# A dense block's second product by seven block products instead of eight, with the halves of its middle layer outermost

## The chip, the core and the metric

The kernel runs on one core of a Trainium2 chip. The metric is the device time of one execution in microseconds. The engines of the core are TensorE (PE: matrix products; PEld is its loading of weights), VectorE (DVE), ScalarE (ACT), GpSimd (POOL) and SyncE (SP), which here only starts DMA transfers. Each engine works through its own queue in program order and waits at semaphores for the others.

## What is computed

Two layers, each an attention block and a dense block, on 2048 rows of 640 numbers in float32; both layers use the same weights:

```
def _A_ref(x, wqkv, wo):            # 32 heads of 20
    q, k, v = heads of (x @ wqkv)
    p = softmax(q k^T * 20 ** -0.5)
    return (p v, heads side by side) @ wo

def _B_ref(x, w1, b1, w2, b2):      # w1: 640 x 1536, w2: 1536 x 640
    h = x @ w1 + b1
    r = where(h > 0, h, 0)
    return (r * r) @ w2 + b2

x = x + _A_ref(layernorm(x), wqkv, wo)
x = x + _B_ref(layernorm(x), w1, b1, w2, b2)
x = x + _A_ref(layernorm(x), wqkv, wo)
x = x + _B_ref(layernorm(x), w1, b1, w2, b2)
```

## The kernel before, in words

Every matrix product of float32 numbers is made of three products: a number is split in a high part, rounded for TensorE (type `F32R`), and a low part, the rest; high x high, high x low and low x high are added up (`THREE`). A split (`split_to`, L269 and L270) is a copy on ScalarE that rounds, and a subtraction on VectorE that gives the rest. The weights are split once, on GpSimd (`pool_hi`, `pool_lo`, L284 and L289), during the attention of the first layer: `prep_job` is called at three of each 16 steps of attention, and the split weights go to DRAM and are loaded again in each layer (`Split`).

The order of work on each engine is the order in which the program writes the instructions down (`manual_schedule`). What belongs to something else than the product in hand is written in between by hand: the dense block calls `side()` after each piece of its work, and each call takes one entry off the list `steps`, which `layer` fills from `plan`.

The **dense block** (`mlp`) is called once for each of four blocks of 512 rows (`qb`). The rows come normalised, transposed and split: `xnt`, five tiles. The middle layer of 1536 columns is worked on in two halves (`fh`) of six chunks of 128. For each half:

- First product: for each of six chunks 15 matmuls of 512 columns (`chain`, L306), ScalarE adds the bias and cuts below zero (L1363), VectorE squares (L1364), and the square is split (L269, L270) into one tile `h`.
- During the first half, the four tiles of 128 rows of `x_mid` are loaded and GpSimd adds the bias `b2` to them (L1370).
- Second product: for each of four row tiles and two halves of the 640 output columns, 6 chunks x 3 matmuls of 320 columns (L1378) into one bank of PSUM, which VectorE then adds to the row tile (L1389). After the second half the row tile is stored.

So the work goes block by block, and both halves of the middle layer follow each other for one block. I call the work of one block and one half a group; there are eight in each layer. All of the second product's weights (`w_2`, 16 tiles) and the first's (`w_1`, 15 tiles) stay loaded. Tiles come from an arena of 42 (`NSLOT`), and rows and intermediate results from a pool of 11 (`NX`). PSUM has 8 banks, used in turn (`ps_all`).

Beside this, by way of `plan`, the next block's rows are **turned**: `turn_out` loads its four row tiles, takes their statistics (VectorE, L257 and L258; GpSimd adds and takes the power, L260 and L261), normalises (L265), transposes blocks of 32 (L1318) and stores them to `d_t`; `turn_in` loads them transposed and splits them (L1334 on ScalarE, L1335 on VectorE). In the first layer the results of the dense block are turned too, for the next layer's attention (`ahead`).

What comes ahead of the dense block, `add_heads`, multiplies the heads by `wo` (L306) and stores `x_mid`; meanwhile the weights of the dense block are loaded, and block 0 is turned.

## Time and profile before

| | us |
|---|---|
| median of 3 runs | 3478.88 (3478.14 to 3479.41) |
| the profiled execution | 3476.63 |
| its span in the profile | 3474.8 |
| dense block of the first layer, in the span | 1414.1 to 1746.4 |
| dense block of the second layer, in the span | 3139.2 to 3471.5 |

How to read the views that follow. The page begins with the busy time of each engine, its share of the span and its instructions. A group of instructions by line shows: the line, the engine, the operation, what it writes and reads, shapes, the count; then busy time and the mean length of one in ns; then the idle time of the engine just before these instructions and what ended it ("<-" is the releaser). A row of the timeline is: start, length, engine, line, operation, tiles, how many instructions are merged in it, and in brackets the idle time before it with its releaser. A row of the chain of waits is: start, length, engine, what, how many. A row of a table of stretches is: from and to, length, then the busy time and the number of instructions of PE, PEld, DVE, ACT and POOL, the clock that TensorE was granted (1.00 is full), the busy share of the DMA engines and GB/s.

### The profile page before, as it was taken

How to read it: one execution, taken by the hardware profiler on the slowest of the kernel's cores; microseconds unless marked ns; L12 is line 12 of the kernel's file. 1: busy time of each engine (PE TensorE's matmuls, PEld its weight loads, DVE VectorE, ACT ScalarE, POOL GpSimd, SP SyncE). 2: the span in 40 equal slices, each digit the busy share in tenths (PEclk: the TensorE clock that was granted, in tenths of full speed). 3: DMA queues.
4: the chain of work that ended last, by engine and by line, in shares of the span. 5: the costliest groups of instructions: out<-in, count | busy, mean ns of one | idle time of the engine just before them, and what ended most of it. 6: DMA issues, size and time to landing. Idle time of an engine off the chain costs nothing.

```text
span 3474.8 us, 69900 instructions
## 1 busy us (share of the span) xinstructions
PE 3458.5 (100%) x26490; PEld 2178.2 (63%) x26490; DVE 2745.0 (79%) x5085; ACT 2595.7 (75%) x4170; POOL 814.8 (23%) x940
## 2 busy tenths in 40 slices
PE   9999999999999999999999999999999999999999
PEld 7897444444444446999989964444444444479998
DVE  8888999999999992456568889999999999834443
ACT  3778999999999994222237799999999999932221
POOL 6531444221121121111153201221121121111110
PEclk9999999999999999999999999999999999999999
DMA  9866555322211146734477552222232111376230
GB/s 309 281 232 185 173 163 162 119 62 80 67 52 44 38 121 214 251 106 108 137 269 260 192 154 78 69 79 70 65 83 58 51 48 43 119 245 221 80 83 36
DMA packets 377138, 452.24 MB, mean 130 GB/s; under 512 B 176612, under 2 KB 223716, under 8 KB 376800
## 3 DMA queue, kind: packets, MB, share of 16 engines
q1 hardware_dynamic: 375984, 445.40, 41.9%
q8 instruction: 208, 3.41, 0.4%
q10 hardware_dynamic: 816, 2.36, 0.2%
q14 instruction: 130, 1.06, 0.1%
HBM read 273.34 MB, written 174.30 MB: 129 GB/s over the span
## 4 chain that ended last, share of the span: by engine, by line
PE 97%; DMA 1%; DVE 1%; issue 0%; ACT 0%; POOL 0%; SPq 0%; DVEq 0%; POOLq 0%; ACTq 0%
PE banks L635 29%; PE banks L494 19%; PE banks L621 14%; PE banks L306 13%; PE banks L344 11%; PE banks L1378 10%; PE banks L1219 0%; PE banks L421 0%; ACT e L1226 0%; DVE bst L257 0%; SPq L76 0%; DMA x<-d_x 0%; DMA d_m<-mr 0%; DMA o<-d_r 0%; DMA b_t<-in_B_b_dram 0%
## 5 line engine op out<-in xcount | busy, mean ns | idle before, releaser
L506 DVE TENSOR_REDUCE mx<-banks 128x1 f32<-128x512 f32 x2096 | 1428.7, 686 | 136.0 <-PE banks L494 30.5
L494 PE MATMUL banks<-k,q 60*128 60x512 f32 (+1 forms) x4488 | 1311.3, 370 | 1.9 <-DVE v L390 1.9
L494 PEld LDWEIGHTS banks<-k,q 60*128 60x128 f32 x4488 | 714.5, 184 | 832.0 <-DVE mx L541 725.9
L629 ACT ACTIVATE e<-banks 128x512 f32<-128x512 f32 x1988 | 1195.4, 602 | 13.2 <-PE banks L621 2.2
L635 PE MATMUL banks<-e,vg 128*32 128x512 f32 x8192 | 1093.5, 606 | 1.5 <-ACT e L1226 1.5
L621 PE MATMUL banks<-q,k 62*128 62x512 f32 x3968 | 1072.5, 421 | 0.6 <-DVE mx L562 0.6
L631 ACT ACTIVATE e<-banks 128x1024 f32<-128x1024 f32 x990 | 1007.9, 1018 | 0.0
L541 DVE TENSOR_REDUCE mx<-banks 128x2 f32<-128x512 f32 x928 | 633.0, 682 | 3.4 <-PE banks L494 3.4
L621 PEld LDWEIGHTS banks<-q,k 62*128 62x128 f32 x3968 | 580.3, 184 | 53.8 <-ACT e L629 52.8
L562 DVE CUSTOM_DVE_ANT_0 rl<-banks,rl 128x512 f32<-128x512 f32 x536 | 349.7, 689 | 78.8 <-PE banks L494 60.1
L1363 ACT ACTIVATE r<-banks,b_t 128x512 f32<-128x512 f32 x96 | 66.1, 689 | 416.4 <-PE banks L306 415.0
L344 PE MATMUL banks<-xnT,wqk 64*128 64x512 f32 x2400 | 372.5, 393 | 0.3 <-ACT mark_t L346 0.3
L554 ACT ACTIVATE rl<-banks 128x512 f32<-128x512 f32 x538 | 295.4, 595 | 102.2 <-PE banks L494 85.0
L1378 PE MATMUL banks<-w,h 128*128 128x320 f32 x2304 | 340.4, 309 | 0.0
L1378 PEld LDWEIGHTS banks<-w,h 128*128 128x128 f32 x2304 | 339.2, 188 | 1.2
L306 PE MATMUL banks<-xnT,w 128*128 128x512 f32 x1440 | 329.4, 389 | 0.0
L635 PEld LDWEIGHTS banks<-e,vg 128*32 128x32 f32 x8192 | 161.7, 108 | 258.7 <-issue 254.9
L344 PEld LDWEIGHTS banks<-xnT,wqk 64*128 64x128 f32 x2400 | 294.0, 186 | 30.5 <-issue 2.3
L306 PEld LDWEIGHTS banks<-xnT,w 128*128 128x128 f32 x1440 | 269.7, 188 | 55.2
L284 POOL CAST mr<-nt 128x32 fp32r<-128x32 f32 x64 | 13.4, 210 | 1096.2 <-DVE nt L588 1096.2
L679 POOL TENSOR_TENSOR few<-few,minus_t 128x16 f32<-128x16 f32 x62 | 179.8, 2900 | 189.4 <-DMA few<-d_s 175.1
L344 PE MATMUL banks<-wv,xnT 64*128 64x320 f32 x1920 | 209.8, 308 | 0.8 <-ACT mark_t L346 0.8
(90 smaller groups left out, 2343.4 us busy)
## 6 DMA issues: line engine op xcount, KB each, us to landing
q<-d_qk SPq DMA_DIRECT2D x240, 240.0 KB
d_qk<-ev SPq DMA_DIRECT2D x80, 512.0 KB
k<-d_qk SPq DMA_DIRECT2D x152, 240.0 KB
x<-d_x SPq DMA_DIRECT2D x84, 320.0 KB
d_qk<-ev SPq DMA_DIRECT2D x80, 256.0 KB
d_o<-ot SPq DMA_DIRECT2D x248, 80.0 KB
ot<-d_o SPq DMA_DIRECT2D x38, 512.0 KB
d_v<-v SPq DMA_DIRECT2D x32, 512.0 KB
```

The source lines that it names most:

```text
L306: nc.tensor.matmul(dst, a, b, start=(n == 0), stop=(n == last))
L344: m = nc.tensor.matmul(ch["dst"][:, :width], *pair, start=first, stop=last)
L494: return nc.tensor.matmul(dst, q_t[t][b : b + 60, p, sub * P : (sub + 1) * P], k_t[t // NQB, c][b : b + 60, p, keys], start=True, stop=True,)
L506: nc.vector.tensor_reduce(maxima(t)[:, 2 * par + p, sub, c : c + 1], dst, axis=AX.X, op=ALU.max)
L541: r = nc.vector.tensor_reduce(maxima(t)[:, p : p + 3 : 2, sub, c if not half else column(t, p, sub)], bank.rearrange("q (r k) -> q r k", r=2),
L554: nc.scalar.activation(res, dst, AF.Relu)
L562: nc.vector.tensor_tensor_reduce(out=r, in0=dst, in1=r, scale=1.0, scalar=LEAST, op0=ALU.add, op1=ALU.max, accum_out=maxima(t)[:, 2 * par ...
L621: nc.tensor.matmul(dst, k_t[t // NQB, kt // 4][b : b + 62, p, (kt % 4) * P : (kt % 4 + 1) * P], q_t[t][b : b + 62, p, :], start=True, stop ...
L629: nc.scalar.activation(es[h], dst, AF.Exp, scale=SCALE)
L631: nc.scalar.activation(es[pair], banks[:, 1:3, :], AF.Exp, scale=SCALE)
L635: nc.tensor.matmul(acc[32 * h : 32 * h + 32, :], v_t[t // NQB, kt // 8][:, kt % 8, 32 * h : 32 * h + 32], es[h], start=(kt == 0), stop=(kt ...
L1378: nc.tensor.matmul(dst[:, :HALF], hs[f][:, hx, i * P : (i + 1) * P], w_2.piece(at_2(f0 + f, hw, hf)), start=(f == 0 and (hx, hw) == THREE[0]),
```

## The change

The second product of each group is seen as a product of 2 x 2 blocks: the 512 rows in two halves of 256, the six chunks in three and three, the 640 output columns in 320 and 320. Seven products of blocks (the variant with 4 additions on the left and 4 on the right) replace the eight.

- **Weights** (`Seven` in place of `Split` for `w_2`): for each pair of chunks (f, f + 3) GpSimd makes the four sums of quarter blocks and splits seven operands instead of four, in three calls of `prep_job`; 14 tiles of three pieces for each half of the middle layer go to DRAM. Each half's 14 tiles are loaded in each layer.
- **Left operands** (`left_operands`): after the second chunk of a pair, four additions of 256 columns, on GpSimd for pairs 0 and 1, on VectorE for pair 2, then the splits of a11 (256 columns), of h (the second chunk, 512), of s1 and of s2 (512 each). The first chunk's other half is not split.
- **The product**: three pairs of banks are opened with pairs 0 and 1 of products 0, 1 and 2; then pair 2 of each, and products 3 to 6 are added onto these banks. After each product VectorE adds the bank to the part of the rows where it belongs: 14 additions in a group instead of 8.
- **Order**: `fh` is now the outer loop and the block the inner one. So the rows after the first half are stored to DRAM (`d_half`) and loaded again in the second half; the normalised rows (`xnt`) are stored to `d_xn` and loaded again for the second half (`again`), which does not turn them a second time; only 8 tiles of `w_1` are loaded at the start, the other seven in the last group of the first half, as well as the other half's `w_2`.
- **Turning**: block 1 is turned out during `add_heads`, block 2 during block 0's group of the first half, block 3 during block 1's. In the first layer, blocks 0 to 2 of the result are turned during blocks 1 to 3 of the second half, each row tile after chunks 0, 2 and 4.

The diff, cut to its core:

```
+    class Seven:
+        n = 14
+        wide = 3 * HALF
...
+        def prepared(self, fh, f, top, low):
+            b11, b12 = top[:, :HALF], top[:, HALF:]
+            b21, b22 = low[:, :HALF], low[:, HALF:]
...
+            for dst, a, b in ((t1, b12, b11), (t2, b22, t1), (t3, b22, b12), (t4, b21, t2)):
+                nc.gpsimd.tensor_sub(dst, a, b)
+            halves(1, two(), t1)
+            yield
...
-        + [("2", f) for f in range(NF)]
+        + [("2", f) for f in range(NF // 2)]
...
-    def mlp(qb, xnt, x_mid, x_dst, side, last):
+    def mlp(fh, qb, xnt, x_mid, x_dst, side, last):
...
+        def left_operands(p, r, h):
+            eng = nc.vector if p == 2 else nc.gpsimd
...
+            a11, a21, a12, a22 = r[:, :w], r[:, w:], h[:, :w], h[:, w:]
+            eng.tensor_add(s[:, 0, 0, :], a21, a22)
+            eng.tensor_sub(s[:, 0, 1, :], s[:, 0, 0, :], a11)
+            eng.tensor_sub(s[:, 1, 0, :], a12, s[:, 0, 1, :])
+            eng.tensor_sub(s[:, 1, 1, :], a11, a21)
+            split_to(a[:, 0, :], a[:, 1, :], a11)
+            for x, y in (("h", h), ("s1", s[:, 0]), ("s2", s[:, 1])):
+                x = ops[x, p]
+                y = y if y is h else y.rearrange("p a t -> p (a t)")
+                split_to(x[:, 0, :], x[:, 1, :], y)
+        for n in range(6):
+            p, low = divmod(n, 2)
+            f = fh * 6 + p + 3 * low
...
+            r = xtile("r")[:, :QB]
+            nc.scalar.activation(r, dst, AF.Relu, bias=b1_t[:, f : f + 1])
+            nc.vector.tensor_mul(r, r, r)
+            if low:
+                left_operands(p, top, r)
...
+            if 1 <= n <= 4:
+                x = row_tile(d_half if fh else x_mid, qb * 4 + n - 1)
+                if not fh:
                     nc.gpsimd.tensor_add(x, x, b2_t)
...
+            side()
+        xnt.clear()
+        side()
+        LEFT = (("a", 0), ("s1", 0), ("h", 0), ("s1", w), ("s2", 0), ("s2", w), ("h", w))
...
+        sums = [[ps_all("y") for u in range(2)] for _ in range(3)]
+        for j in range(3):
+            for u in range(2):
+                part(sums[j][u], j, u, range(2), True, False)
+        ADDS = ((0, 0, 0), (1, 1, 1), (2, 0, 0), (0, 0, 1), (1, 0, 1), (0, 1, 1), (0, 1, 0))
+        for j, (bank, lower, hf) in enumerate(ADDS):
+            for u in range(2):
+                dst, i = sums[bank][u], 2 * lower + u
+                part(dst, j, u, (2,) if j < 3 else range(3))
+                x, c = xs[i], slice(hf * HALF, (hf + 1) * HALF)
                 nc.vector.tensor_add(x[:, c], dst[:, :HALF], x[:, c])
...
+                elif j in (4, 6):
+                    dma(nc.sync, (x_dst if fh else d_half)[r0 : r0 + P, :], x)
...
+                side()
...
+            if qb == NQB - 1:
+                w_2.past(j)
+                if not fh:
+                    for n in (2 * j, 2 * j + 1):
+                        w_2.load(1, n)
...
+            if not fh and qb + 1 < NQB:
+                put(turn_in(d_t[(qb + 1) % 2], to(new)), 6, 13, 14, 15, 16, 17)
+                plan[20].append(lambda: [dma(nc.sync, d_xn[qb + 1, k], new[k]) for k in range(KD)])
+            elif (fh, qb) != (1, NQB - 1):
+                plan[7].append(lambda: again((qb + 1) % NQB))
+            if not fh and qb + 2 < NQB:
+                put(outs.pop(0), -1, -1, 0, 0, 2, 2, 4, 13, 14)
...
+            if ahead and fh and qb:
+                at = (6, 8, 9) if qb + 1 == NQB else (13, 15, 16)
+                put(turn_out(d_t[1 + qb], rows_of(x_e, qb - 1)), -1, 0, 0, 2, 2, 4, 4, *at)
```

(`put(gen, i)` runs the generator's next step at `plan[i + 1]`: entry 0 comes ahead of the first chunk, entries 1 to 6 after the six chunks, 7 ahead of the second product, 8 to 21 after its 14 parts.)

More of the change, by code (lines that the diff above doesn't have):

```diff
@@ L699, in tile_layers @@
         + [("1", j) for j in range(NF)]
-        + [("2", f) for f in range(NF)]
+        + [("2", f) for f in range(NF // 2)]
     )
+    sevens = []
     def prep_job():
+        if sevens:
+            if next(sevens[0], "end") is None:
+                return
+            sevens.clear()
         if raws:
@@ L1477, in to, with again @@
                 return get
[L1479 to L1490 removed]
+            def again(qb):
+                new.extend(new_rows())
+                for k in range(KD):
+                    dma(nc.sync, new[k], d_xn[qb, k])
@@ new lines, in layer @@
+            if not fh and qb + 1 < NQB:
[5 more added lines that the diff above has]
+                put(outs.pop(0), -1, -1, 0, 0, 2, 2, 4, 13, 14)
+            if not fh and qb + 3 < NQB:
+                outs.append(turn_out(d_t[(qb + 1) % 2], rows_of(x_m, qb + 3)))
+                put(outs[0], 18)
@@ new lines, in layer @@
+            if not fh and qb + 1 == NQB:
+                for n in range(7):
+                    plan[(0, 0, 2, 4, 4, 4, 5)[n] + 1].append(lambda n=n: w_1.load(8 + n))
+            if ahead and fh and qb:
+                at = (6, 8, 9) if qb + 1 == NQB else (13, 15, 16)
+                put(turn_out(d_t[1 + qb], rows_of(x_e, qb - 1)), -1, 0, 0, 2, 2, 4, 4, *at)
+            if ahead and fh and qb + 2 >= NQB:
+                for tb, at in enumerate((13, 6, 15)):
+                    if (tb == 0) == (qb + 2 == NQB):
+                        xt_[tb] = []
+                        sub = nc.gpsimd.tensor_sub if tb == 2 else nc.vector.tensor_sub
+                        d = 6 if tb == 1 else 3
+                        put(turn_in(d_t[2 + tb], to(xt_[tb]), sub), at, *[min(at + d + i, 20) for i in range(5)])
@@ L1491, in layer @@
+            if ahead and fh and qb + 1 == NQB:
                 for n in range(5):
-                    plan[20 + n].append(lambda n=n: w_qk.load(n))
+                    plan[15 + n].append(lambda n=n: w_qk.load(n))
             steps.extend((lambda p=p: [f() for f in p]) for p in plan)
-            mlp(qb, xnt, x_m, x_e, side, not ahead)
+            side()
+            mlp(fh, qb, xnt, x_m, x_e, side, not ahead)
             xnt = new
-            if qb + 1 < NQB:
-                all_steps()
+            all_steps()
@@ L1498, in layer @@
         steps.clear()
         w_1.drop()
-        w_2.drop()
     def second():
```

221 lines of the change are left out of this document (127 added, 94 removed).

## The prediction

> **What bounds the kernel now.** I read the page first, then the groups of instructions by line, then the chain of waits in order of time over the two dense blocks.
>
> ```profile
> span 3474.8 us, 69900 instructions
> PE 3458.5 (100%) x26490; PEld 2178.2 (63%) x26490; DVE 2745.0 (79%) x5085; ACT 2595.7 (75%) x4170; POOL 814.8 (23%) x940
> ```
> ```profile
> L1378 PE MATMUL banks<-w,h 128*128 128x320 f32 x2304 | 340.4, 309 | 0.0
> L306 PE MATMUL banks<-xnT,w 128*128 128x512 f32 x1440 | 329.4, 389 | 0.0
> L1389 DVE TENSOR_TENSOR x<-banks,x 128x320 f32<-128x320 f32 x128 | 61.0, 480 | 120.6 <-PE banks L1378 120.5
> ```
> ```profile
> 1455.64 20.43 PE banks L306 x90
> 1476.06 21.11 PE banks L1378 x144
> 1497.18 20.43 PE banks L306 x90
> ```
>
> TensorE is busy for the whole span; its idle time before both products of the dense block is 0.0 us. The chain shows the unit of work: for one block of 512 rows and one half of the middle layer (a "group"; there are 16 in the two layers) 90 matmuls of the first product take 20.43 us and 144 of the second 21.11 us, so one of the second takes 21.11 / 144 = 0.1466 us. Whatever takes matmuls out of a group shortens the kernel, as long as the other engines still deliver in time. How near are they?
>
> ```profile
> 1497.20:1538.70 41.50, 41.50 (x235) 37.97 (x235) 25.28 (x40) 7.76 (x12) 10.44 (x12) 1.00 0.38 96
> 1538.70:1580.30 41.60, 41.60 (x236) 38.05 (x235) 24.30 (x46) 10.46 (x17) 4.40 (x8) 1.00 0.53 127
> ```
>
> These are two groups of one block (columns: length, then PE, PEld, DVE, ACT, POOL busy, clock, DMA share, GB/s). VectorE works 24 to 25 of 41.5 us, ScalarE 8 to 10, the DMA engines are half free. So VectorE is the engine to watch.
>
> **What is removed.** Seven block products over 3 + 3 chunks, 2 row tiles and 3 terms make 7 x 2 x 3 x 3 = 126 matmuls instead of 144. 18 x 0.1466 x 16 groups = 42.2 us. By this alone the profiled execution's 3476.6 us would become 3434.4. (The median of the runs shown, 3478.9, lies 2.3 us above the profiled execution; I add that at the end.)
>
> **What is added on the path.** The second product now starts with 36 matmuls that need only chunk pairs 0 and 1 (3 products, 2 row tiles, 2 pairs, 3 terms): 36 x 0.1466 = 5.28 us. After that it needs the pieces of pair 2. Counted from a group's start, TensorE wants them at 20.43 + 5.28 = 25.7 us. The pieces come out of VectorE's queue, which runs in program order. I therefore work through that queue. The prices:
>
> ```profile
> 1500.69 0.69 ACT L1363 ACTIVATE r<-banks,b_t 128x512 f32<-128x512 f32 x1 [19.86 <-PE banks L306]
> 1502.13 0.62 ACT L269 CAST h<-r 128x512 fp32r<-128x512 f32 x1 [0.76 <-DVE r L1364]
> ```
> ```profile
> 1501.41 0.69 DVE L1364 TENSOR_TENSOR r<-r 128x512 f32<-128x512 f32 x1 [3.70 <-ACT r L1363]
> 1502.79 1.70 DVE L270 TENSOR_TENSOR h<-r,h 128x512 fp32r<-128x512 f32 x1 [0.69 <-ACT h L269]
> 1504.76 1.70 DVE L1364 TENSOR_TENSOR r<-r 128x512 f32<-128x512 f32 x1 [0.28 <-ACT r L1363]
> 1507.15 1.29 DVE L270 TENSOR_TENSOR h<-r,h 128x512 fp32r<-128x512 f32 x1 [0.69 <-ACT h L269]
> 1508.36 2.05 DVE L1364 TENSOR_TENSOR r<-r 128x512 f32<-128x512 f32 x1
> 1525.64 0.21 DVE L258 BATCH_NORM_AGGREGATE mv<-bst 128x2 f32<-128x12 f32 x1
> 1526.78 0.61 DVE L265 TENSOR_SCALAR x<-x,mv 128x640 f32<-128x640 f32 x1 [0.58 <-POOL mv L261]
> 1527.42 0.85 DVE L1318 STREAM_TRANSPOSE y<-x 128x640 f32<-128x640 f32 x1
> ```
> ```profile
> 1439.64 6.18 POOL L1370 TENSOR_TENSOR x<-x,b_t 128x640 f32<-128x640 f32 x4 [54.06 <-DMA x<-d_x]
> 1502.37 7.48 POOL L1370 TENSOR_TENSOR x<-x,b_t 128x640 f32<-128x640 f32 x4 [44.28 <-DMA x<-d_x]
> ```
> ```profile
> L289 POOL TENSOR_TENSOR w<-raw,w 128x256 fp32r<-128x256 f32 x6 | 4.4, 737 | 0.0
> ```
> ```profile
> 1442.55 0.89 DVE L257 BATCH_NORM_STATS2 bst<-x 128x6 f32<-128x320 f32 x2 [5.15 <-DMA x<-d_x]
> 1443.60 0.45 DVE L1389 TENSOR_TENSOR x<-banks,x 128x320 f32<-128x320 f32 x1
> ```
>
> A square or a subtraction of 512 columns costs VectorE 0.69 us alone. While GpSimd runs its four bias additions (1502.37 to 1509.85), the same operations take 1.29 to 2.05: each waits until GpSimd's current instruction is over and then takes its 0.69. The two engines exclude each other, instruction by instruction; the addition out of PSUM at 1443.60, amid GpSimd's other run of four, keeps its 0.45. For 256 columns I estimate 0.42 on VectorE (from 0.69 for 512 and 0.45 for 320); GpSimd takes 0.74 (the 256-column row). One row tile of turning (statistics 0.89 + 0.21, a wait of about 0.9 from there to the normalisation through GpSimd, 0.61, 0.85) holds VectorE's queue for 3.45 us.
>
> The new left operands of one pair: four additions of 256 columns, then four splits (a of 256 columns; h, s1, s2 of 512), each a ScalarE copy and a VectorE subtraction. For pairs 0 and 1 the additions are GpSimd's. s2's subtraction can't come before four additions (4 x 0.74), a copy of 0.62 and its own 0.69: 4.3 us and the hand-overs after the second square, though VectorE works only 0.42 + 3 x 0.69 = 2.5 us. With GpSimd's additions and the subtractions excluding one another I get 5.2 us. In the first half of the middle layer GpSimd also owes four bias additions (6.18 / 4 = 1.55 us each with no rival), which slip in ahead of s2's subtraction and of the next square. For pair 2 VectorE does all: 4 x 0.43 + 0.42 = 2.1 us from square 5 to the first piece. Squares become possible 0.8 us after each 3.4 us chain: at 4.2, 7.6, 11.0, 14.4, 17.8, 21.2.
>
> So VectorE's queue runs (us from the group's start):
> - **plain** (second half, no turning: 5 groups). Square 1 done 8.3, pair 0 13.5, squares 2 and 3 15.1, pair 1 20.3, square 5 21.9, pair 2's first piece 24.0, under 25.7. Stall 0; the other pieces follow 0.65 apart against 0.88 of matmuls.
> - **second half with turning** (first layer, blocks 1 to 3: 3 groups). Three row tiles are turned after squares 0, 2 and 4: square 0 4.9, tile 8.35, square 1 9.0, pair 0 14.2, square 2 14.85, tile 18.3, square 3 18.95, pair 1 24.15, square 4 24.85, tile 28.3, square 5 28.95, piece 31.05. Stall 5.35, with 0.4 for s1 behind it 5.7. 3 x 5.7 = 17 us.
> - **first half, no turning** (blocks 2 and 3 of both layers: 4 groups). Square 1 8.3; the bias additions push pair 0 to 15.0 and square 2 to 17.2; square 3 17.85, pair 1 24.5, a bias addition, square 5 27.35, piece 29.45. Stall 3.75 + 0.4. 4 x 4.1 = 16 us.
> - **first half with turning** (blocks 0 and 1: 4 groups). Square 1 9.0, pair 0 15.7, square 2 17.85, tile 21.3, square 3 21.95, pair 1 28.65, square 4 30.8, statistics 31.9, square 5 32.55, piece 34.65. Stall 8.95 + 0.4. 4 x 9.3 = 37 us.
>
> After that VectorE owes 14 additions instead of 8 (0.45 each, 6.3 us), a last tile and, in most first-half groups, five subtractions of 0.69: 11 of some 18 us, so the debt does not pass into the next group.
>
> **A stalled TensorE slows down.** Before the change its longest waits come at the ends of attention:
>
> ```profile
> 3032.20:3034.90 2.70, 0.00 (x1) 0.03 (x1) 0.00 (x0) 0.44 (x1) 0.00 (x0) 0.78 0.12 18
> 3034.90:3038.10 3.20, 3.20 (x12) 0.92 (x12) 0.00 (x0) 1.94 (x2) 0.00 (x0) 0.50 0.50 159
> 3038.10:3041.00 2.90, 2.90 (x18) 1.03 (x14) 0.69 (x1) 1.97 (x3) 0.00 (x0) 0.58 0.01 3
> 1310.00:1313.30 3.30, 3.27 (x14) 0.98 (x14) 0.00 (x0) 1.94 (x2) 0.00 (x0) 0.50 0.52 159
> ```
>
> After 2.7 us of nothing the granted clock was 0.50 for 3.2 us and 0.58 for 2.9 more (2.8 us lost); the other such wait cost 3.3 us at 0.50, 1.65 lost. I charge 1.7 to the seven groups whose stall is over 5 us: 12 us; the ends are 0 and 11 x 2.8 = 31.
>
> The Trainium skill ("TensorE: Matmul & The Clock Gate", what is actually happening) says that a whole idle window of about 3.4 us halves the clock, and that a busy window of that length restores it. The 2.7 us gaps here did it already. By the page the 4.1 us stalls would count too, at 3.4 / 2 = 1.7 each: an estimate of 19 us instead of 12.
>
> **What lies beside other work.** Attention hides the preparation of the weight sums on GpSimd, with TensorE busy throughout and GpSimd idle for more than half:
>
> ```profile
> 313.00:697.00 384.00, 384.00 (x3033) 168.34 (x3029) 362.97 (x600) 381.83 (x573) 144.53 (x183) 1.00 0.52 155
> ```
>
> ```profile
> L289 POOL TENSOR_TENSOR w<-raw,w 128x320 fp32r<-128x320 f32 x24 | 20.9, 872 | 1.9
> L284 POOL CAST w<-raw 128x320 fp32r<-128x320 f32 x24 | 10.8, 450 | 17.9 <-DMA raw<-in_B_w_dram 9.2 <-PE banks L635 8.7
> ```
>
> Per pair of chunks it is now 4 subtractions and 7 splits of 320 columns, 4 x 0.87 + 7 x 1.32 = 12.7 us, six times, instead of 24 x 1.32 in all: 45 us more. I charge 0, because nobody needs the sums before the dense block; uncovered they would cost those 45 us.
>
> The new transfers (normalised rows stored and read back, 2.6 MB; half sums, 1.3 MB) add 3.9 MB to a group, 100 GB/s to the 96 to 127 above. The first group of the dense block shows that this is bearable:
>
> ```profile
> 1414.10:1455.60 41.50, 41.50 (x235) 37.97 (x235) 18.29 (x34) 7.86 (x12) 8.35 (x10) 1.00 0.81 298
> ```
>
> It moved 298 GB/s and TensorE missed nothing. The second half's weights (seven times 0.96 MB) are asked for half a group ahead. I charge 0 here as well. The exception is the start of each layer's dense block:
>
> ```profile
> 0.74 3.33 DMA x<-in_A_x_dram
> ```
> ```profile
> 1414.01 3.08 SPq L76 DMA_DIRECT2D d_x<-x  x4
> 1417.98 10.58 SPq L76 DMA_DIRECT2D w<-d_w  x11
> ```
>
> The first group (from 1414.1) now turns block 2 at once, and its rows are asked for behind these four stores (over at 1417.1) and four of such loads (0.96 us each), and take 3.3 us to land: 10 us into the group, where VectorE wants them at 0.5. Square 0 then ends at 13.6, not 4.9, and all behind it comes 9 us later. Seven loads of the first product's weights, which stand ahead of them today, are gone, so the queue may be short and this may cost nothing. Between 0 and 9 I take 3 in each layer: 6 us.
>
> **The sum.** 3476.6 - 42.2 + 17 + 16 + 37 + 12 + 6 = 3522.4 us, and 2.3 to the median of the runs: 3525.
>
> **The rivals.**
> - *The cover holds.* If the queue on VectorE runs shorter than I make it, TensorE stays full and the gain arrives: 3434.4 + 2.3 = 3437, with a few us for the starts. For it: VectorE is busy only about 34 of 39 us even in the fullest groups (4.1 squares, 7.5 splits, 1.7 additions, 6.3 sums, 10.2 turning, 3.4 splits of turned rows). Against it: the limit lies not in the group's total but in the first 25.7 us, and even with nothing lost between VectorE and GpSimd I count 29.5 us there in the groups with turning in the second half. It decides at 25.7 us. 0.13.
> - *GpSimd's additions hardly get in the way.* If its short instructions slip between VectorE's, pairs 0 and 1 take 4.4 us: the plain groups and those of the first half without turning stall 0, those of the first half with it about 1.8, those of the second half with it 4.5: 4 x 1.8 + 3 x 4.5 = 21 us. 3476.6 - 42.2 + 21 + 2.3 = 3458. Against it: the rows at 1502 to 1510, where no operation slipped in. 0.14.
> - *It is worse.* All eleven stalls slow the clock by the dearer row (31 instead of 12 us) and the rows come late by the full 9 us twice (18 instead of 6): 3525 + 31 = 3556. 0.14.
> - That the change doesn't save the matmuls isn't likely: the loops of the second product are written out for seven products.
>
> **How the numbers follow.** My forecast has 0.54, own range 3498 to 3540 (2 us of stall more or less in each of the eleven groups). Faster holds the first two rivals, 0.27; between the second and the forecast lies 0.05 for no change; slower is 0.54 + 0.14 = 0.68. About 0.2% (7 us) is what a measurement of this kernel can tell from no change. The range, 3440 to 3555, leaves out half of the first rival and half of the last and the tails beyond.
>
> **What would show it.** The second product should have 2 x 1008 matmuls at the same 309 ns. Right: TensorE has gaps of 3 to 9 us before the second product's 37th matmul, released by VectorE's subtraction of pair 2's a, in 11 of 16 groups and none in the plain ones; VectorE's squares follow ever later after their ScalarE activations in groups with turning; subtractions of 512 columns average well over 0.8 us; the granted clock drops behind the gaps. Wrong: 18.5 us for each second product throughout (then the cover held), or gaps that a DMA releases, or gaps ahead of the first product (then the rows read back are the trouble, which I charged at nothing).

## The result, and the profile after

The changed kernel takes 3571.0 us (median of three executions, 3570.1 to 3574.8) against 3478.7 for the kernel before: ratio 1.0268 (1.0248 to 1.0288). Left out, here and below, are executions in a slower state with a lower granted clock: a fourth one of the changed kernel (6183.5 us; with it the median is 3572.9) and two of the variant without the bias (3641.9 and 3702.1 us). The changed kernel is slower, as forecast, but by 92 us, and the forecast was 46 us (3525, range 3440 to 3555). The page of its profiled execution (3574.8 us) begins so:

```profile
span 3573.0 us, 70330 instructions
PE 3461.2 (97%) x26202; PEld 2163.7 (61%) x26202; DVE 2864.7 (80%) x5341; ACT 2640.3 (74%) x4266; POOL 975.4 (27%) x1128
```

TensorE has 288 matmuls fewer (18 x 16) and yet is no less busy than before (3461.2 against 3458.5), and now it idles too: 3573.0 - 3461.2 = 112 us, where before it was 16. The groups of instructions by line show where (the second product is now L1481, in three groups by left operand; its additions are L1500, the squares L1455, the first product L361):

```profile
L361 PE MATMUL banks<-xnT,w 128*128 128x512 f32 x1440 | 335.6, 394 | 8.2 <-DVE xnT L1404 8.2
L1481 PE MATMUL banks<-w,hs 128*128 128x320 f32 x1152 | 189.7, 321 | 2.0 <-ACT hs L324 1.3 <-DVE hs L325 0.3
L1481 PE MATMUL banks<-w,h 128*128 128x320 f32 x576 | 98.4, 322 | 2.3 <-DVE x L1500 2.3
L1481 PE MATMUL banks<-w,ha 128*128 128x320 f32 x288 | 60.8, 349 | 79.7 <-DVE ha L325 51.6 <-ACT ha L324 28.0
L1500 DVE TENSOR_TENSOR x<-banks,x 128x320 f32<-128x320 f32 x224 | 104.7, 486 | 79.6 <-PE banks L1481 78.3
L1455 DVE TENSOR_TENSOR r<-r 128x512 f32<-128x512 f32 x96 | 80.6, 844 | 68.6 <-ACT r L1454 67.9
```

There are 1152 + 576 + 288 = 2016 matmuls in the second product, as planned, but they last 321 to 349 ns instead of 309, and 79.7 us of waiting stand ahead of those that read `ha`, the split of a11, which opens each pair of chunks (L324 is now the copy of a split, L325 its subtraction). The forecast had named gaps at this place. The table of stretches for the second layer, one row for each group, shows which groups have them:

```profile
3204.20:3280.10 75.90, 48.17 (x219) 41.23 (x218) 41.14 (x77) 13.71 (x24) 18.49 (x22) 0.78 0.75 225
3280.10:3328.90 48.80, 41.62 (x218) 36.77 (x217) 33.34 (x61) 12.99 (x23) 17.57 (x20) 0.97 0.62 181
3328.90:3371.80 42.90, 41.18 (x219) 36.97 (x218) 26.14 (x41) 13.12 (x23) 14.59 (x12) 0.96 0.43 154
3371.80:3413.90 42.10, 39.74 (x219) 35.42 (x218) 24.00 (x36) 10.51 (x18) 15.08 (x12) 1.00 1.01 388
3413.90:3452.80 38.90, 38.90 (x218) 35.37 (x217) 19.39 (x36) 10.61 (x18) 7.50 (x8) 1.00 0.51 190
```

The fifth row is a plain group: 38.9 us, busy throughout, clock 1.00. So a group without trouble gains 41.5 - 38.9 = 2.6 us, as reckoned. The first group of the layer lasts 75.9. It is the same in the first layer (74.7). TensorE's timeline in the second layer's first group:

```profile
3207.01 0.96 PE L361 MATMUL banks<-xnT,w 128*128 128x512 f32 x3 [2.42 <-DVE xnT L1404]
3209.78 22.35 PE L361 MATMUL banks<-xnT,w 128*128 128x512 f32 x86 [1.82 <-DVE xnT L1404]
3236.82 0.90 PE L1481 MATMUL banks<-w,ha 128*128 128x320 f32 x2 [4.68 <-ACT ha L324]
3240.75 0.63 PE L1481 MATMUL banks<-w,ha 128*128 128x320 f32 x1 [3.03 <-DVE ha L325]
3246.84 0.90 PE L1481 MATMUL banks<-w,ha 128*128 128x320 f32 x2 [5.46 <-ACT ha L324]
3253.40 2.24 PE L1481 MATMUL banks<-w,ha 128*128 128x320 f32 x7 [5.65 <-DVE ha L325]
```

The first product waits twice, 4.2 us in all, for splits of block 0's own turned rows (`xnT`), which were ready too late. Then it runs, and the second product has nothing: pair 0 should have been there long before. VectorE and SyncE's queue in the same group:

```profile
3232.20 0.89 DVE L312 BATCH_NORM_STATS2 bst<-x 128x6 f32<-128x320 f32 x2 [18.28 <-DMA x<-d_x]
3235.68 0.65 DVE L1455 TENSOR_TENSOR r<-r 128x512 f32<-128x512 f32 x1
```
```profile
3201.03 5.63 SPq L76 DMA_DIRECT2D d_t<-y  x4
3206.76 0.45 SPq L76 DMA_DIRECT2D d_x<-x  x1
3207.31 1.90 SPq L76 DMA_DIRECT2D w<-d_w  x4
3209.30 6.69 SPq L76 DMA_DIRECT2D d_t<-y  x4
3216.09 0.45 SPq L76 DMA_DIRECT2D d_x<-x  x1
3216.64 3.06 SPq L76 DMA_DIRECT2D d_t<-y  x4
3219.80 1.45 SPq L76 DMA_DIRECT2D d_x<-x  x3
3221.34 2.67 SPq L76 DMA_DIRECT2D w<-d_w  x4
3224.07 1.29 SPq L76 DMA_DIRECT2D x<-d_x  x2
```

VectorE finishes what is left of the heads and of block 0's splits at 3213.9. Its next task is the turning of block 2, and it idles for 18.28 us until those rows land at 3232.2. The first square follows at 3235.7, 31 us into the group; the forecast had it end at 4.9, and at 13.6 if the rows came as late as it thought possible. SyncE asks for those rows only at 3224.1, 20 us into the group, because ahead of them stand the stores of block 1's turned rows: in these rows, four of them hold the queue for 3 to 7 us.

### The profile page after: what moved, and what is told of

It is laid out like the page before. It is cut to its first block, busy times and chain, and to the rows that moved or that the text cites. A ratio compares the mean times of both kernels' runs of the same rounds, so it can differ in the third digit from the quotient of the medians.

```text
span 3573.0 us, 70330 instructions
## 1 busy us (share of the span) xinstructions
PE 3461.2 (97%) x26202; PEld 2163.7 (61%) x26202; DVE 2864.7 (80%) x5341; ACT 2640.3 (74%) x4266; POOL 975.4 (27%) x1128
## 5 line engine op out<-in xcount | busy, mean ns | idle before, releaser
L361 PE MATMUL banks<-xnT,w 128*128 128x512 f32 x1440 | 335.6, 394 | 8.2 <-DVE xnT L1404 8.2
L361 PEld LDWEIGHTS banks<-xnT,w 128*128 128x128 f32 x1440 | 273.0, 190 | 66.3 <-DVE xnT L1404 10.1
L399 PEld LDWEIGHTS banks<-wv,xnT 64*128 64x128 f32 x1920 | 202.2, 186 | 1.8 <-ACT mark_t L401 1.4
L549 PE MATMUL banks<-kd,q 60*128 60x512 f32 x538 | 193.4, 397 | 0.0
```

Of the source, the lines that this page charges most:

```text
L361: nc.tensor.matmul(dst, a, b, start=(n == 0), stop=(n == last))
L399: m = nc.tensor.matmul(ch["dst"][:, :width], *pair, start=first, stop=last)
L549: return nc.tensor.matmul(dst, q_t[t][b : b + 60, p, sub * P : (sub + 1) * P], k_t[t // NQB, c][b : b + 60, p, keys], start=True, stop=True,)
```

## The experiments

The lengths of the groups tell the runs apart, so here they are for all kernels, in us, from a group's first matmul to the next one's (read off TensorE's timeline of the profiled execution; the last one to the end of its last matmul). Each line: four groups of the first half, four of the second.

```
                       first layer                               second layer
before                 41.5 41.5 41.5 41.5 | 41.5 41.5 41.5 41.7   the same
changed                74.7 48.0 41.3 43.6 | 38.9 46.6 47.1 48.6   75.9 48.9 42.8 42.1 | 38.9 38.9 38.9 39.1
e1_rows_later          77.1 49.8 41.3 42.1 | 38.9 46.1 46.8 48.6   77.0 51.0 41.3 43.6 | 38.9 38.9 38.9 39.1
e2_results_later       73.8 47.6 41.3 43.4 | 38.9 45.8 49.1 48.3   75.6 48.2 42.8 42.1 | 38.9 38.9 38.9 39.1
e3_no_bias             69.4 43.8 38.9 38.9 | 38.9 47.1 45.8 48.6   70.8 43.8 38.9 38.9 | 38.9 38.9 38.9 39.1
e4_order_alone         75.0 48.0 41.5 41.5 | 41.5 43.3 43.3 48.4   74.0 48.3 41.5 41.9 | 41.5 41.5 41.5 41.7
e5_all_on_vector       70.8 44.4 39.5 40.3 | 38.9 43.0 41.5 46.7   73.5 45.5 39.5 40.4 | 38.9 38.9 38.9 39.1
e6_other_queue         67.5 48.4 41.3 43.6 | 38.9 46.6 47.1 48.6   68.6 48.7 41.3 43.5 | 38.9 38.9 38.9 39.1
e7_one_ahead           62.3 51.1 51.4 42.0 | 38.9 46.1 46.8 48.6   61.0 50.8 50.4 44.0 | 38.9 38.9 38.9 39.1
e8_bias_later          72.1 45.4 39.6 38.9 | 38.9 46.7 45.6 48.6   73.3 45.5 39.6 38.9 | 38.9 38.9 38.9 39.1
e9_early_rows          51.9 50.5 51.1 43.8 | 38.9 46.5 47.0 48.6   52.9 52.9 51.3 42.5 | 38.9 38.9 38.9 39.1
e10_vector_and_bias    70.2 42.7 39.7 38.9 | 38.9 42.8 41.5 47.0   69.8 43.6 39.8 38.9 | 38.9 38.9 38.9 39.1
e11_three_together     45.9 43.5 42.1 38.9 | 38.9 41.6 43.0 45.4   46.5 42.7 42.2 38.9 | 38.9 38.9 38.9 39.1
e12_all                49.7 39.8 39.8 38.9 | 38.9 39.6 45.2 44.9   51.1 40.3 39.9 38.9 | 38.9 38.9 38.9 39.1
e13_rows_first         46.2 40.1 39.5 38.9 | 38.9 38.9 39.1 41.1   45.7 39.6 39.3 38.9 | 38.9 38.9 38.9 39.1
e14_early_rows_alone   61.7 48.5 41.3 43.6 | 38.9 46.6 47.1 48.6   60.5 48.6 41.3 43.6 | 38.9 38.9 38.9 39.1
e15_eight_products     41.5 42.6 41.8 41.5 | 41.5 41.5 41.5 41.7   41.5 48.0 42.5 41.5 | 41.5 41.5 41.5 41.7
e16_later_splits       44.6 40.2 39.7 38.9 | 38.9 39.2 38.9 40.8   42.6 40.2 39.2 38.9 | 38.9 38.9 38.9 39.1
```

**e1_rows_later: Block 2's turning behind the first product, in the first group only.**

```
-                put(outs.pop(0), -1, -1, 0, 0, 2, 2, 4, 13, 14)
+                put(outs.pop(0), *(range(7, 16) if qb == 0 else (-1, -1, 0, 0, 2, 2, 4, 13, 14)))
```

> Only block 2's turning in the first group of each layer moves, from ahead of the chunks to behind the first product. Theory A (VectorE stands at the rows of block 2, asked for too late, and everything in its queue behind it waits; 36 us lost in each layer's first group): the first groups fall from 75 us to about 50 us (4 to 5 us from the late end of turning block 0 remain, and 4 from the bias additions), so some 50 us less: 3523. Rival B (the stall of the first group is the left operands' own queue, as in the other groups): only the 9 us of VectorE's three turned row tiles go, 2 x 9 us or less: 3555.

3574.5 us, 1.0278 (1.0263 to 1.0293): both expectations missed. VectorE no longer waits for block 2's rows, but GpSimd's addition of the bias comes after 20 us of idling, and pair 1's additions stand behind it in its queue. GpSimd's timeline ("issue": the profile shows no releaser; SyncE asked for the rows that it adds to from 3230.9 on, 10 us ahead of it):

```profile
3240.88 3.02 POOL L1466 TENSOR_TENSOR x<-x,b_t 128x640 f32<-128x640 f32 x2 [20.13 <-issue]
```

So it isn't these two row tiles alone: the rows that the bias is added to, for which SyncE is asked behind them, come late as well.

**e2_results_later: The results' turning moved behind the first product (second half, first layer).** One row tile after square 0, three behind (`at` becomes `range(7, 14)`, in block 3's group `range(6, 13)`).

```
-                put(turn_out(d_t[1 + qb], rows_of(x_e, qb - 1)), -1, 0, 0, 2, 2, 4, 4, *at)
+                put(turn_out(d_t[1 + qb], rows_of(x_e, qb - 1)), -1, 0, 0, *at)
```

> Only the turning of the first layer's results moves: one row tile still after square 0, three behind the first product. Theory A (VectorE's queue ahead of pair 2 is too long by two row tiles): the three groups of 46.6, 47.2 and 48.5 us fall to about 39 to 40, 23 us less: 3550. Rival B (these groups wait for transfers or for GpSimd, or VectorE has no room behind the first product either): under 8 us less, the stall comes back in the second product's additions.

3575.2 us, 1.0279 (1.0264 to 1.0294): the rival. The 5 us gap ahead of pair 2 goes, and TensorE's timeline has another in its place, between the products, where a bank is written again whose addition VectorE has put behind the turning:

```profile
1697.24 4.88 PE L1481 MATMUL banks<-w,hs 128*128 128x320 f32 x18 [4.62 <-DVE x L1500]
```

**e3_no_bias: Without the bias.** GpSimd's additions of `b2` are taken out.

> Leaves out the addition of b2 to the rows (32 additions on GpSimd). Theory A (GpSimd's bias additions shut VectorE's subtractions and squares out and delay s2): the first half's groups without turning (41.3 to 43.6 us) fall to 38.9, those of block 1 (48.0 and 48.8) by 2 to 4 us: 18 to 22 us less in all, 3552. Rival B (GpSimd's own four additions for the left operands are the limit): under 5 us less.

This variant leaves out a part of the computation, so it is read by its groups and not by a ratio. Two executions take 3535.4 us (the profiled one) and 3540.2: some 33 us less, where 18 to 22 were expected. The groups of the first half without turning come down to 38.9, without any stall, block 1's from 48 to 43.8, and also the first ones by 5, which the expectation had left out. Three rows of the changed kernel's timeline show what GpSimd's additions did there: one of VectorE in block 2's group, then one of GpSimd and one of VectorE in block 1's.

```profile
3343.44 2.65 DVE L1455 TENSOR_TENSOR r<-r 128x512 f32<-128x512 f32 x2
```
```profile
3296.76 3.08 POOL L1466 TENSOR_TENSOR x<-x,b_t 128x640 f32<-128x640 f32 x2 [3.25 <-DMA x<-d_x]
```
```profile
3300.65 0.61 DVE L320 TENSOR_SCALAR x<-x,mv 128x640 f32<-128x640 f32 x1 [4.12 <-POOL mv L316]
```

Two squares take 2.65 us while GpSimd adds (one alone takes 0.69). And where GpSimd waits for rows (3.25), the short powers of the next row tile's statistics wait behind it in its queue, and VectorE, for 4.12 us, for them.

**e4_order_alone: The order alone.** The halves outermost with all its stores, loads and turning, but eight products of the split chunks, as before.

```
-                left_operands(p, top, r)
+            split_to(ops[n][:, 0, :], ops[n][:, 1, :], r)
...
-        for j, (bank, lower, hf) in enumerate(ADDS):
+        for hf in range(2):
+            for i in range(0 if hf else 2, 4):
```

> Halves outermost with all its stores, loads and turning, but the eight block products of before (144 matmuls, six splits, eight additions in a group; the sums of weights are made and loaded, and b12 takes the place of one of them). Theory A (order and turning schedule cost most): the first groups lose about 30 us each as VectorE stands at the late rows, the other 14 groups are near 41.5 us: 3479 + 60 to 66 = 3540 to 3545. Rival B (the seven products' left operands cost nearly all): 3480 to 3490.

3576.0 us, 1.0284 (1.0268 to 1.0299), far above both expectations: the order alone costs 97 us, and the seven products seem to bring nothing. The first groups take 75 here as well, so the sums and splits of the seven products aren't what makes them long.

**e5_all_on_vector: All additions of the left operands on VectorE.**

```
-            eng = nc.vector if p == 2 else nc.gpsimd
+            eng = nc.vector
```

> The left operands' additions of all three pairs on VectorE, none on GpSimd. If what costs the groups is that GpSimd's additions and VectorE's subtractions exclude one another, a pair takes VectorE about 4.2 us (4 x 0.42 and 2.5) instead of the 5.2 or more between the two engines, and the groups outside the plain ones come 1 to 3 us earlier each: about 3553 us. The rival is that GpSimd relieves VectorE: then its queue, 1.7 us longer for each of two pairs, makes 11 groups up to 3.4 us longer: up to 3610. In both the first group of each layer stays over 70 us.

3536.7 us, 1.0172 (1.0157 to 1.0188): 34 us less than the changed kernel, and 16 less than the 3553 expected. VectorE does more, and is ready earlier: what was meant to relieve it held it up. Whether by exclusion alone, this run does not show. In the changed kernel GpSimd's four additions of one pair take 3.8 us, and VectorE's own for pair 2 (0.42 to 0.43 each) 1.7, so the splits behind GpSimd's also start later:

```profile
3289.60 0.79 POOL L1434 TENSOR_TENSOR s<-r,r 128x256 f32<-128x256 f32 x1 [2.25 <-DVE r L1455]
3290.47 1.07 POOL L1435 TENSOR_TENSOR s<-s,r 128x256 f32<-128x256 f32 x1
3291.61 0.74 POOL L1436 TENSOR_TENSOR s<-r,s 128x256 f32<-128x256 f32 x1
3292.31 1.20 POOL L1437 TENSOR_TENSOR s<-r 128x256 f32<-128x256 f32 x1
```

**e6_other_queue: Block 1's stores on ScalarE's queue.**

```
-                    nc.sync,
+                    q,
...
-                out_1 = turn_out(d_t[1], rows_of(x_m, 1))
+                out_1 = turn_out(d_t[1], rows_of(x_m, 1), nc.scalar)
```

> Only the queue of block 1's sixteen stores of turned rows in the stage of the heads changes: ScalarE's instead of SyncE's; the bytes and their pieces stay. Theory: SyncE is the bottleneck of the first groups, because such stores hold it for 2 to 8 us per four (37.7 us for eight times four in the second layer, 17.2 for four times four before), so that the rows of block 2 are asked for 20 us into the group. Without the sixteen, these rows are asked for near the group's start, land some 8 us later, and each first group loses about 20 us of its 75: about 3533 us. Rival: the DMA engines themselves are full (share 0.86 to 1.06 there), then the rows land as late as now whoever asks, and the groups stay at 70 to 75: about 3570.

3576.3 us, 1.0284 (1.0267 to 1.0301); the first groups come to 67.5 and 68.6, and start 8 and 11.5 us later. ScalarE's queue (first fence) and TensorE's:

```profile
3194.88 20.08 ACTq L76 DMA_DIRECT2D d_t<-y  x12
```
```profile
3215.73 2.37 PE L361 MATMUL banks<-xnT,w 128*128 128x512 f32 x4 [11.39 <-ACT xnT L1403]
```

The stores hold the queue here too: ScalarE issued twelve in 20 us, its split of block 0's rows came behind them, and TensorE waited 11.4 us for it. The delay moved; as a test of SyncE it says little.

**e7_one_ahead: One block ahead.** Block 1 is turned in block 0's group, and so on, not in the heads; the splits of its turned rows come two parts later.

```
-        outs = [turn_out(d_t[0], rows_of(x_m, 2))]
+        outs = [turn_out(d_t[1], rows_of(x_m, 1))]
...
-                out_1 = turn_out(d_t[1], rows_of(x_m, 1))
...
+                put(outs.pop(0), -1, -1, 0, 0, 2, 2, 4, 4, 5)
...
-                put(outs.pop(0), -1, -1, 0, 0, 2, 2, 4, 13, 14)
...
```

> Block 1 is not turned during the heads, but in block 0's group, block 2 in block 1's, block 3 in block 2's: one block ahead, as the kernel before does it. Both the theory of SyncE's queue and that of full DMA engines expect the first groups to fall, to 45 to 55 us, since the stage of the heads loses sixteen stores of small pieces and four loads; block 2's group of the first half now turns and grows from 41 to 43 us to about 48. In all about 3540 us. If the first groups stay above 65, the added turning is not what delays them, and the normalised rows stored at the group's start and the loads behind them are.

3564.5 us, 1.0253 (1.0238 to 1.0268), not the 3540 expected. The first groups fall by 12 and 15 us, not by 20 to 30, and the two behind them rise to 50 and 51: all four row tiles are now turned in the first product.

**e8_bias_later: The bias later.** GpSimd adds it in the middle of the second product.

```
-                if not fh:
-                    nc.gpsimd.tensor_add(x, x, b2_t)
...
+            if not fh and j in (1, 3):
+                for x in xs[2:] if j == 1 else xs[:2]:
+                    nc.gpsimd.tensor_add(x, x, b2_t)
```

> GpSimd adds the bias b2 to the row tiles in the middle of the second product instead of during the first; all is computed. By the theory that its additions keep VectorE and GpSimd from the left operands, the groups of the first half come out as where the bias was left out: 38.9 without turning, about 44 in block 1, 70 in block 0: about 3539 us in all. Rival: the additions then meet the second product's own additions and the splits of the turned rows on VectorE, and come back there as gaps between the products: 3560 or more.

3545.4 us, 1.0198 (1.0183 to 1.0213): 26 us less than the changed kernel, most of what leaving it out gave (38.9 and 39.6 without turning). Little comes back in the second product: in the first layer, waits of 1.79 us in block 1's group and 0.46 in block 2's for VectorE's additions.

**e9_early_rows: One block ahead, and SyncE asked earlier.** On top of the one-ahead variant: `next(outs[0])`, which asks for two row tiles, stands ahead of the last block's heads; six loads of weights and the stores to `d_xn` come inside the group.

> The variant that turns one block ahead (first groups 62.3 and 61.0 us, the two groups behind them 50 to 51), and in it only SyncE's order around the first group: block 1's rows are asked for before the last block of the heads, the last six loads of the second product's weights and the stores of block 0's normalised rows come inside the group. Theory: what is left of the first group's excess over the next ones is the rows' lateness (asked for 3.4 us into the group, landed after 12). Then the first groups come down to the 51 of the others: 3564 - 21 = 3543 us. Rival: it is the DMA engines' load at this place; then the first groups stay at 58 or more and the time at 3555 or more.

3549.1 us, 1.0213 (1.0196 to 1.0230). The first groups come to 51.9 and 52.9, the length of those behind them (50.5 to 52.9). So in this variant what set a layer's first group apart was SyncE's lateness.

**e10_vector_and_bias: Additions on VectorE and the bias later, together.**

> The changed kernel with two things together: the left operands' additions all on VectorE, and the bias added by GpSimd in the middle of the second product. Theory: both take GpSimd's work out of the way of the first product, and overlap in part: groups of the first half without turning 38.9, block 1 about 43, second half with turning as with the additions alone (43.0, 41.5, 46.7), the first groups still 68 to 70, as their rows are late in SyncE's queue: about 3523 us. If they were the same gain it would be no better than 3536.

3525.0 us, 1.0140 (1.0125 to 1.0155), as expected (3523): 46 us from the two, where each alone gave 34 and 26. The first groups stay at 70.

**e11_three_together: These with one ahead and SyncE's order.**

> All of it: additions on VectorE, bias late, one block ahead, SyncE's order mended. Theory: each of the first three groups of a layer about 45, the fourth 38.9, the second half 38.9 and (first layer) 43.0, 41.5, 46.7: about 345 and 330 us for the dense blocks instead of 388.8 and 365.4, and some 7 us less in the heads: about 3487 us. Rival: the queue of SyncE holds the later turning groups up (stores of turned rows in 14 us for eight), then 50 each and 3515.

3479.7 us, 1.0011 (1.0002 to 1.0020): 7 us better than expected, and within 0.2% of the kernel before.

**e12_all: And the squares on ScalarE, with the row tiles turned where VectorE has room.**

```
-            nc.vector.tensor_mul(r, r, r)
+            nc.scalar.activation(r, r, AF.Square)
...
-            if 1 <= n <= 4:
+            if n >= 2:
...
```

> The same, and besides the squares on ScalarE, two row tiles turned together ahead of the first square, the third between pairs 0 and 1, the fourth between pairs 1 and 2. By the model of VectorE's queue its pair 2 then has its first piece at 24.0 to 24.8 us after the group's start, where TensorE needs it at 25.7: no stall in any group, 16 x 39 to 40 us, about 3450 us, faster than both kernels. Rival: the rows turned so late are stored late, SyncE's stores (2 to 8 us per four) put off the loads for the next block, and each of six groups loses 3 us or more at its end: 3470 or above.

3474.2 us, 0.9995 (0.9985 to 1.0004), not the 3450 expected but within the rival's time. The groups with turning reach 39.8, but the first ones went up to 50. The row tiles that the second product adds to are asked for with the third to sixth chunk here, behind the stores of turned rows, and VectorE waited for them (one of two such waits in the second layer's first group, the other 4.17 us):

```profile
3176.49 0.49 DVE L1532 TENSOR_TENSOR x<-banks,x 128x320 f32<-128x320 f32 x1 [4.08 <-DMA x<-d_x]
```

**e13_rows_first: These row tiles asked for first.**

```
-            if n >= 2:
-                x = row_tile(d_half if fh else x_mid, qb * 4 + n - 2)
+            if n < 2:
+                for i in range(2):
+                    xs.append(row_tile(d_half if fh else x_mid, qb * 4 + 2 * n + i))
...
```

> The variant with everything (3474 us), and in it the row tiles that the second product adds to are asked for after chunks 0 and 1 of each group, ahead of the stores of turned rows in SyncE's queue; the normalised rows of block 0 are stored earlier in the group; one set of splits at the end of the first layer comes later. Theory: the waits of 4.08 and 4.17 us for these rows in the first groups and of 1.6 in the last one, and that of 5.4 for a split, are the queue's order and go: first groups 51 to about 41, the last two of the first layer 45 to about 41: about 3446 us, faster than both kernels. Rival: the DMA engines are full there and the rows land late anyway: first groups 47 or more, 3465.

3457.4 us, 0.9947 (0.9933 to 0.9960): faster than both kernels, though 11 us short of the expectation: the first groups come to 46, not 41. The last two groups of the first layer lose nearly all of their stall (39.1 and 41.1).

**e14_early_rows_alone: The changed kernel with the requests alone earlier.** The same edit to SyncE's order as above, with block 1 still turned in the heads.

> The changed kernel with nothing but the requests in another order: the first two row tiles of block 2 are asked for before the last block of the heads, six loads of weights and the stores of block 0's normalised rows come inside the first group; block 1 is still turned during the heads. If the lateness of these two row tiles alone makes the first groups 75 us, they fall to the 48 of block 1's group and the time to about 3521 us. If block 1's stores in the heads hold SyncE itself for the first 15 us of the group, the other rows (block 2's last two, and the four that GpSimd adds the bias to) stay late behind them: first groups 60 or more, 3545 or more.

3541.9 us, 1.0190 (1.0176 to 1.0204), near the second expectation (3545 or more): the first groups lose 13 and 15 us, not 26. SyncE's queue still issues block 1's stores until 3203.2, 17 us into this group (it starts at 3186.4), and the other rows come behind them:

```profile
3192.51 7.41 SPq L76 DMA_DIRECT2D d_t<-y  x4
3200.02 0.45 SPq L76 DMA_DIRECT2D d_x<-x  x1
3200.57 2.61 SPq L76 DMA_DIRECT2D d_t<-y  x4
3203.28 1.49 SPq L76 DMA_DIRECT2D d_x<-x  x3
3204.82 0.74 SPq L76 DMA_DIRECT2D x<-d_x  x1
```

**e15_eight_products: Eight products in the fastest surroundings.** The variant with 3457.4 us, its second product replaced as in the order alone.

> The fastest variant (3457 us, dense blocks 322.8 and 319.2 us) with eight products in place of seven, as in the variant with the order alone: no sums of left operands, the first chunks split like the second, eight additions. Theory: where the other engines deliver in time, the eighteen matmuls are worth their 2.6 us a group (41.5 against 38.9): 16 groups of 41.5 to 42 and first groups of 45: about 3492 us, 35 more. Rival: the surroundings with a full queue hide it, as they did in the changed kernel, where eight products in the same order cost the same as seven: 3465 or less.

3490.9 us, 1.0039 (1.0026 to 1.0052). So here the seven products do bring 3490.9 - 3457.4 = 33.5 us of the 42, where the surroundings hold the groups up far less. (Its list, with the 48.0, is that of the slowest of five executions, 3496.9 us.)

**e16_later_splits: The splits of the first group later.** The five splits of block 1's rows there move from behind parts 9 to 13 of the second product to behind parts 11 to 14, the stores to `d_xn` behind the sixth chunk.

> The fastest variant, and in the first group of each layer the splits of the next block's turned rows come two parts later and the stores of block 0's normalised rows behind the last of the turned ones. Theory: the 5 us gap ahead of the last product there is VectorE's queue waiting for these rows, with six additions behind the wait: first groups 46 to about 42, 3457 to about 3449 us. Rival: the gap moves to the start of the next group's first product, which needs these rows: 3455 or more.

3452.7 us, 0.9933 (0.9921 to 0.9946): the shortest time of all, 23 us below the kernel before, though its interval overlaps that of the variant it starts from (0.9933 to 0.9960). The first groups come to 44.6 and 42.6. The one in the second layer, and then the first 27 us of the same group in the changed kernel:

```profile
3128.40:3171.00 42.60, 39.44 (x218) 35.65 (x218) 28.86 (x61) 16.88 (x29) 9.47 (x12) 0.99 0.98 315
```
```profile
3204.20:3231.30 27.10, 22.86 (x90) 18.09 (x88) 8.28 (x17) 2.00 (x3) 1.08 (x2) 0.87 0.97 284
```

The DMA engines are as full here (0.98 of the time, 315 GB/s) as in the changed kernel while VectorE waits for its rows (0.97, 284 GB/s), and yet this group takes 42.6 us and that one 75.9. So full DMA engines alone do not make the group long. This variant differs in more than SyncE's order; what that order does is shown by the two variants with earlier requests (e9_early_rows, e14_early_rows_alone).

## Why the prediction was wrong

By its own steps, against the ideal of a plain group (38.9 us, and 39.1 to the end of the last one: 38.91 x 16 = 622.6), in the profiled executions, both layers together:

| step of the forecast | forecast, us | measured, us |
|---|---|---|
| 18 matmuls fewer in a group | -42.2 | -42.4 (665.0 - 622.6) |
| second half, no turning (5 groups) | 0 | 0 |
| second half with turning (3), with its slow clock | 17 + 5 | 7.7 + 8.2 + 9.7 = 26 |
| first half, no turning (4) | 16 | 2.4 + 4.7 + 3.9 + 3.2 = 14 |
| first half, block 1 (2), with its slow clock | 2 x 11.0 = 22 | 9.1 + 10.0 = 19 |
| first half, block 0 (2): 9.3, clock 1.7, late rows 3 | 28 | 35.8 + 37.0 = 73 |
| outside the dense blocks | 0 | 9 |

The gain came as reckoned. The fourteen groups that are not the first of a layer did so in sum, 59 us for a forecast of 60, but that is luck in part: two errors in it cancelled, as the paragraph on the clock says. The forecast's mechanism, that the pieces of pair 2 come too late out of VectorE's queue, is right: there are gaps ahead of them, which the subtraction of pair 2's a ends, in eleven groups and in none of the plain ones. They last 1.66 to 5.09 us, not 3 to 9.

**The step that failed** is the last term of the sum, the late rows: "Seven loads of the first product's weights, which stand ahead of them today, are gone, so the queue may be short and this may cost nothing. Between 0 and 9 I take 3 in each layer: 6 us." The first group was given 14 us in all, and measured 36 and 37: some 22 us a layer more. So 9 was no upper bound. The forecast looked at the loads that leave SyncE's queue, and not at what the change puts in: block 1's turning in the heads, sixteen more stores in pieces of 128 bytes. In the second layer, the stores of turned rows from the heads into the first group hold the queue for 7.93 + 2.57 + 2.88 + 6.83 + 2.15 + 5.63 + 6.69 + 3.06 = 37.7 us, where before it was 17.2:

```profile
3096.37 7.98 SPq L76 DMA_DIRECT2D d_t<-y  x4
3105.50 3.10 SPq L76 DMA_DIRECT2D d_t<-y  x4
3109.73 3.37 SPq L76 DMA_DIRECT2D d_t<-y  x4
3114.22 2.78 SPq L76 DMA_DIRECT2D d_t<-y  x4
```

The difference is about the 20 us after which block 2's rows were asked for. That alone proves nothing, as SyncE also waited for other engines on the way (25.1 us for VectorE's additions in the heads). The variants show it: earlier requests alone take 13 to 15 us off the first groups, and with the stores out of the heads too, 23, which is about the surplus. The forecast had named two signs of being wrong that came: "gaps that a DMA releases" (it meant TensorE's; here it is VectorE's 18.28 us, with TensorE behind it), and "gaps ahead of the first product", the 4.2 us above, which it charged at nothing. It is not the rows read back that are late there, as it had supposed, but block 0's own.

**The slow clock** was charged too low, and the waits too high. TensorE's busy time in the stretches of the two dense blocks is 335.6 and 326.4 us; beyond 16 x 38.91 that is 39.5 us (19.2 of them in the two first groups), for a forecast of 12 with an end of 31. Nearly all of it is the slow clock: the two stalled groups with a clock of 1.00 have 0.7 and 0.8 us of it. In the other nine stalled groups it is 20 where 8.5 was charged, and the waits themselves were 39 us, not 52: the model of VectorE's queue was some 13 us too long. Short gaps can count too. These rows of stretches lie behind a gap of 1.66 us (block 2's group, second layer) and one of 5.09 (block 1's of the second half, first layer):

```profile
3356.90:3360.50 3.60, 3.52 (x16) 3.26 (x17) 3.60 (x8) 2.89 (x6) 0.00 (x0) 0.75 0.00 0
3360.50:3363.50 3.00, 3.00 (x17) 3.00 (x17) 1.40 (x4) 0.00 (x0) 0.00 (x0) 0.74 0.00 0
```
```profile
1694.80:1698.00 3.20, 3.20 (x12) 3.20 (x13) 3.08 (x7) 0.25 (x1) 0.00 (x0) 0.50 0.29 44
1698.00:1701.20 3.20, 3.20 (x18) 3.20 (x17) 1.53 (x4) 0.00 (x0) 0.00 (x0) 0.72 0.00 0
```

The Trainium skill ("TensorE: Matmul & The Clock Gate", what's actually happening) asks for a whole idle window of some 3.4 us; the forecast's estimate by it, 19 us, was short too. The trace differs: behind the gap of 1.66 us, 1.7 us were lost at 0.75 and 0.74. Four groups of the changed kernel, those of blocks 2 and 3 in the first half, have a gap of 1.66 to 1.73 us ahead of pair 2. Two left the group's mean clock at 0.96, two at 1.00, and what sets them apart is open. TensorE's timeline has one of each, block 2's and block 3's in the second layer:

```profile
3356.92 0.85 PE L1481 MATMUL banks<-w,ha 128*128 128x320 f32 x4 [1.66 <-DVE ha L325]
...
3400.52 0.85 PE L1481 MATMUL banks<-w,ha 128*128 128x320 f32 x4 [1.72 <-DVE ha L325]
```

**GpSimd.** That its additions and VectorE's work get in each other's way was rightly seen: moving the bias gives 26 us, moving the additions of the left operands 34, both 46; the forecast's second rival had put it at 17 + 16 + 37 - 21 = 49 us of stalls. How much of that is exclusion, and how much the slower additions themselves (3.8 us a pair against 1.7), no run here separates. What the forecast did not see is GpSimd's own queue: additions, bias and the powers of the statistics follow one another in order, so that a bias addition that waits for late rows holds up VectorE's next row tile (4.12 us above). The Trainium skill ("GPSIMD Engine Reference", key points) says that GpSimd shares its paths to the on-chip memory with VectorE and contends with instructions that read two inputs there. The 2.65 us for two squares, each of which reads two, agree.

Of the signs that the forecast named, one was wrong: subtractions of 512 columns average 0.76 and 0.78 us, not "well over 0.8"; the squares average 0.84, but they had 0.81 before the change, so these means tell little. Of the rivals, the third (3556) came nearest, though it was short on both its grounds: the slow clock cost even more than its dearer price (39.5 us against 31), and its rows were late by 9 us at most. Two of the forecast's figures do not add up, and nothing above hangs on them: VectorE's work in the fullest groups comes to 33.2 us, not 34, and 2 us in each of eleven groups would make its own range 3503 to 3547. Not followed up are the 9 us outside the dense blocks: 3 ahead of the first, 6 between the two.

## What to carry to other kernels

- A change that adds DMA is costed by the queue that issues it: what each new transfer holds the queue for while the DMA engines are full, and who is queued behind it. List what the change puts into the queue as carefully as what it takes out, above all where two stages meet.
- Work that is moved to another engine for relief has to be followed through that engine's queue; with the additions on GpSimd, VectorE was later than when it did them all itself.
- Fewer matmuls pay (33.5 us here) only when every group's operands are there in time; a variant that changes the order alone shows beforehand what the surroundings cost.

## What the runs showed of the hardware

- Four stores of one turned row tile held SyncE's queue for 2.0 to 8.0 us. The long ones (over 5 us) lie in stretches where the DMA engines were busy for 0.86 of the time or more, but not all stores there were long (2.15 us at 0.98). On ScalarE's queue twelve took 20.1 us, and its next operation waited.
- Additions out of PSUM keep their length beside GpSimd's work (0.49 us on average in the changed kernel, 0.48 before), whereas a 512-column square went from 0.69 to over 1.3 us.
- A gap of 1.66 us in TensorE's work was followed by a granted clock of 0.75 and 0.74 for 6.6 us; one of 1.72 us was not (1.00).
